# Regrouping the second feed-forward block of a top-k attention kernel, with one matmul reshaped and every rank set anew

## The chip, the cores and the metric

One Trainium2 chip, one of its cores. The metric is the device time of one run in microseconds (us). Five engines work side by side, each through its own list of instructions in a fixed order: PE (matmuls, with weight loads shown as PEld), DVE, ACT, POOL, and SP, which here only issues DMAs.

## The reference, cut to what matters

```python
# q, k, v: (2, 8, 576, 64); 1152 tokens = 9 tiles of 128; d_model 512, d_ff 2048
scores = scale * np.matmul(q, k.transpose(0, 1, 3, 2))
kth = np.partition(scores, -32, axis=-1)[..., -32:-31]
scores = np.where(scores >= kth, scores, -1e9)
attn = softmax(scores)                      # over the 32 that are left
x = np.matmul(attn, v)                      # heads put back: (1152, 512)
h = x @ w_in;  x = (h * np.tanh(softplus(h))) @ w_out      # first block
h = x @ w2_in; out = (h / (1 + np.exp(-h))) @ w2_out       # second block
```

The four weight arrays arrive as float64 and are turned into float32 in the kernel (`convert`), with ACT and POOL; q, k and v are float32.

## The kernel before, in words

The 1152 tokens are nine tiles of 128 rows, and the eight heads are four pairs, so there are 36 pieces of attention (a tile and a head pair), called pairs below and numbered 1 to 36 in the order in which PE turns their weights over. A pair is eight looks for the eight largest scores (L394) and six replacements (L397) on DVE, an exponential on ACT, a mask (L414 on DVE for tiles 0 to 5; L290 or L292 on POOL or DVE for tiles 6 to 8), nine transposes on PE (L439), copies of these out of PSUM (`pt`), and the products with the values (L455 and L457, function `values`). The last chunk of values holds the last 64 keys of each of the two heads, one above the other; a single product with 128 columns (L457) adds it to both heads.

Two feed-forward blocks follow. Each has 16 chunks of `w_in` and 16 of `w_out`. The lists `BLOCK1` and `BLOCK2` say which tiles share a pass over the weights, and how: `'n'` multiplies in float32 as it stands, which the profile shows as two recorded instructions for each product; `'r'` splits each operand into a float32r high part and a rest and adds three products (`passes`). For `'r'` the weights have to be split first (`weight`: a cast L282 or L284 into `ws`, then a subtraction, L290 on POOL or L292 on DVE). The first `'r'` group splits all chunks; some are kept or written to DRAM for the groups behind it, the others are split again by each group. The activations are split by `split_unit`, into a tile named `wide`, a name that the buffers of the float64 weights have too.

What stands when on which engine is not written out. Each step is added to `Plan` with a rank, made from the tables `TILES`, `DUE1`, `DUE2` (when a tile or a group is due), `OFF` (how much earlier or later a kind of step is) and `FLEX`, `FLEX1` (which engine takes a step that two could take). `Plan.emit` takes the steps one by one in the order of rank as their inputs and buffers allow, and so fixes each engine's list. On the chip each engine goes through its list in order and waits where an input is not there yet.

Of the kernel before, what the change touches and what calls it, by code (L numbers as in the profile page):

```python
# [11 lines left out]
F32R = mybir.dt.float32r  # L12
# [14 lines left out]


BLOCK1 = [([0], 'n'), ([1], 'n'), ([2], 'n'), ([3, 4], 'r'), ([5, 6], 'r'), ([7, 8], 'r')]
BLOCK2 = [([0, 1], 'n'), ([2], 'n'), ([3, 4], 'r'), ([5, 6], 'r'), ([7, 8], 'r')]  # L30

TILES = [(19.37, 6.76), (46.36, 14.1), (106.73, 4.63), (204.37, 9.99), (225.06, 11.69), (258.55, 49.85), (345.98,
         18.22), (519.3, 17.23), (461.45, 16.83)]
DUE1 = [(55.53, 32.57), (72.6, 11.18), (185.18, 33.6), (264.74, 3.6), (326.98, 167.36), (749.26, 11.24)]
DUE2 = [(194.98, 61.15), (262.2, 26.21), (504.62, 78.52), (783.18, 203.62), (946.46, 197.95)]

SBUF_BUFS = dict(kraw=1, kk=5, v=5, qraw=2, qs=2, sc=4, rest=1, e=1, pt=2, m8=10, bias=10, den=8, x=3, dt=2, xt=1,
                 wraw=9, ws=8, hs=2, th=1, wide=3, y=2, o=2)
PSUM_BUFS = dict(att=2, misc=1, h=3, y=2)

FLEX = dict(khi=-199.43, klo=-179.86, qhi=-300.0, qlo=65.82, whi=259.95, wlo=-153.31, ghi=-62.92, glo=163.54,
            hs=286.73, mk=-58.0, se=-300.0, den=105.07, y=271.68, sc=-47.47, pt=57.06, dt=-238.16, xlo=98.83)
FLEX1 = dict(khi=245.84, klo=30.36, qhi=-26.57, qlo=179.72, whi=-172.94, wlo=-208.13, ghi=-191.1, glo=300.0, hs=19.48,
             mk=8.23, se=None, den=-282.09, y=None, sc=252.9, pt=None, dt=239.76, xlo=-232.84)
EARLY = 553.02

OFF = dict(kload=578.07, qload=135.46, k=16.71, q=-13.88, sp=314.62, sc=197.87, bias=39.06, e=246.77, tp=342.92,
           pt=330.03, av=-14.23, x=487.41, den=300.22, dw=35.2, dp=222.21, xt=191.17, m=-75.12, cload=96.71,
           cpn=-97.42, cse=5.37, cw=-99.8, cmid=-37.21, wload=572.6, wsplit=-171.63, wstore=206.7, g=-82.77, hs=-40.2,
           y=-31.25, th=709.1)  # L50
# [20 lines left out]
class Plan:  # L71
# [173 lines left out]
def kernel(ctx: ExitStack, tc, qh, kh, va, w1i, w1o, w2i, w2o, out):  # L245
    nc = tc.nc
    NT, DM = out.shape
    NPAIR, D = qh.shape[1], qh.shape[2] // 2
# [94 lines left out]
    def attention(t, p, rank):  # L343
        g, j = group_of[t]
# [3 lines left out]
        pp = parts(t)  # L348
        key = (t, p)
# [99 lines left out]
        def values():  # L449
            av = get(K("av"), lambda: psum("misc", [P, P]))  # L450
            for b, r0, r1 in pp:
                v = T["v", b, p]
                for c in range(NM):
                    for h in range(2):
                        nc.tensor.matmul(av[h * D:h * D + D, r0:r1], lhsT=v[:, h * NM + c, :], rhs=pt()[:, h * (NM + 1) + c, r0:r1],  # L455
                                         start=(c == 0), stop=False, skip_group_check=True)
                nc.tensor.matmul(av[:, r0:r1], lhsT=v[:, 2 * NM:].rearrange("p c e -> p (c e)"), rhs=pt()[:, NM, r0:r1],  # L457
                                 start=False, stop=True, skip_group_check=True)
        add([("pe", 1.35 * len(pp), 0, values)], reads=[K("pt", c) for c in range(0, NB, 3)] + [("v", b, p) for b, _, _ in pp],
            writes=[K("av")], uses=[(K("av"), "ps_misc"), (K("pt"), "pt")] + [(("v", b, p), "v") for b, _, _ in pp],  # L460
            rank=rank + 10.5, boost="av")
        add([("act", 0.11, 0, lambda: nc.scalar.add(den()[:, 0], den()[:, 0], tiny)),
# [182 lines left out]

# [236 lines left out]
```

## Time and profile before

| | |
|---|---|
| Time, median of 3 runs | 653.43 us (652.98 to 654.75) |
| Profiled execution: span from first to last instruction | 654.1 us |
| PE busy | 606.1 us (93%) |
| DVE busy | 539.5 us (82%) |
| ACT busy | 476.3 us (73%) |
| POOL busy | 382.3 us (58%) |
| DMA queue of SP, share of 16 engines | 80.4% |

The profiled execution has no time of its own beside its span; the span is 0.6 us above the median of the runs. Busy shares are means over a program with stages: attention is spread over most of it, and the second block's last groups fill the end. A busy PE may still be a PE that waits inside an instruction, so PE's rate is read from the steps between the starts of its instructions.

### The profile page before, as it was taken

The page shows a single profiled execution, that of the slowest core. Times are in us where ns is not written, and L with a number is a line of the kernel's source. Part 1 is how long each engine was busy: PE and PEld are TensorE (multiplying, and loading weights), DVE is VectorE, ACT ScalarE, POOL GpSimd, SP SyncE. Part 2 cuts the span into 40 slices and gives each one's busy share as a digit, 9 for nine tenths or more (in the row PEclk, how much of TensorE's full clock was granted, in tenths as well). Part 3 has the DMA queues.
Part 4 walks back from the last instruction along what each step waited for, and adds up shares of the span by engine and source line. Part 5 has one row for each costly group of instructions (what it writes and reads, how often), then busy time and mean ns, then how long its engine had stood idle before and what let it go on. Part 6 is the DMA issues. An engine that isn't in the chain of part 4 may idle for free.

```text
span 654.1 us, 13089 instructions
## 1 busy us (share of the span) xinstructions
PE 606.1 (93%) x4536; PEld 537.0 (82%) x4536; DVE 539.5 (82%) x1106; ACT 476.3 (73%) x993; POOL 382.3 (58%) x334
## 2 busy tenths in 40 slices
PE   1298788999999999999999999999999999999997
PEld 1177667999999866668999878999988899999996
DVE  4999999997999999989999979979998234554550
ACT  6799999988699998988978666878777344332321
POOL 6898569761267888987549236556787233322221
PEclk9999967999999999999999999999999999999999
DMA  8987649898789868799999589875876998887752
GB/s 309 293 256 222 197 159 330 312 361 263 204 271 345 276 192 271 268 305 347 389 402 368 151 272 355 316 259 191 272 255 223 374 300 294 278 263 256 246 179 80
DMA packets 85650, 178.34 MB, mean 273 GB/s; under 512 B 8144, under 2 KB 29136, under 8 KB 85584
## 3 DMA queue, kind: packets, MB, share of 16 engines
q1 hardware_dynamic: 85584, 177.50, 80.4%
q8 instruction: 36, 0.59, 0.3%
q14 instruction: 30, 0.25, 0.1%
HBM read 138.94 MB, written 38.54 MB: 271 GB/s over the span
## 4 chain that ended last, share of the span: by engine, by line
PE 53%; DVE 16%; ACT 15%; DMA 7%; issue 4%; POOL 4%; SPq 1%; POOLq 0%; ACTq 0%
PE ps_h L630 20%; PE ps_y L701 12%; PE ps_y L808 11%; DVE m L394 6%; DVE rest L397 5%; ACT ws L505 4%; PE ps_att L378 3%; DMA wraw<-w1i 3%; PE ps_att L439 2%; PE ps_misc L455 2%; ACT wraw L517 2%; ACT pt L282 2%; ACT e L410 2%; DVE e L414 2%; POOL wraw L519 2%
## 5 line engine op out<-in xcount | busy, mean ns | idle before, releaser
L394 DVE MAX8 m<-rest 128x8 f32<-128x576 f32 x216 | 154.4, 745 | 0.1
L397 DVE MATCH_REPLACE8 rest<-m,rest 128x576 f32<-128x576 f32 x144 | 106.2, 741 | 0.0
L509 POOL TENSOR_TENSOR ws<-ws 128x512 int32<-128x512 int32 x64 | 86.7, 1359 | 28.9 <-ACT ws L505 27.2
L378 PE MATMUL ps_att<-kk,qs 128*128 128x288 f32 x320 | 72.8, 346 | 31.6 <-POOL kk L290 24.5
L282 ACT CAST ws<-wraw 128x512 fp32r<-128x512 f32 x93 | 57.4, 621 | 53.8 <-PE ps_h L630 25.3
L519 POOL TENSOR_TENSOR wraw<-wraw,ws 128x512 int32<-128x512 int32 x64 | 85.5, 1346 | 15.9 <-ACT wraw L517 11.0
L505 ACT ACTIVATE ws<-wide,zone 128x512 int32<-128x512 int16 x128 | 94.5, 779 | 0.0
L378 PEld LDWEIGHTS ps_att<-kk,qs 128*128 128x128 f32 x320 | 51.3, 205 | 43.2 <-POOL kk L290 26.0
L292 DVE TENSOR_TENSOR ws<-wraw,ws 128x512 fp32r<-128x512 f32 x65 | 58.9, 924 | 31.3 <-ACT ws L282 30.9
L630 PE MATMUL ps_h<-y,ws 128*128 128x256 f32 x576 | 75.3, 280 | 0.0
L630 PEld LDWEIGHTS ps_h<-y,ws 128*128 128x128 f32 x576 | 73.1, 188 | 2.7
L290 POOL TENSOR_TENSOR ws<-wraw,ws 128x512 fp32r<-128x512 f32 x44 | 57.6, 1318 | 27.3 <-ACT ws L282 14.8
L630 PE MATMUL ps_h<-xt,ws 128*128 128x256 f32 x576 | 72.8, 282 | 0.0
L701 PE MATMUL ps_y<-wide,ws 128*128 128x256 f32 x540 | 71.3, 283 | 0.0
L630 PEld LDWEIGHTS ps_h<-xt,ws 128*128 128x128 f32 x576 | 69.5, 188 | 1.5 <-issue 1.2
L290 POOL TENSOR_TENSOR wide<-th,wide 128x512 fp32r<-128x512 f32 x24 | 31.5, 1313 | 66.7 <-DVE wide L284 65.4
L701 PEld LDWEIGHTS ps_y<-wide,ws 128*128 128x128 f32 x540 | 66.5, 189 | 0.0
L808 PE MATMUL ps_y<-ws,wide 128*128 128x512 f32 x252 | 64.8, 396 | 0.0
L290 POOL TENSOR_TENSOR wide<-hs,wide 128x512 fp32r<-128x512 f32 x24 | 32.0, 1342 | 49.4 <-DVE wide L284 40.2
L439 PE MATMUL ps_att<-ident,e 128*128 128x128 f32 x324 | 52.6, 287 | 6.7 <-DVE e L414 3.9
L701 PE MATMUL ps_y<-hs,wraw 128*128 128x128 f32 x384 | 52.4, 286 | 2.2 <-ACT hs L670 2.2
L394 DVE MAX8 m<-sc 128x8 f32<-128x576 f32 x72 | 52.8, 747 | 1.3 <-ACT sc L282 0.7
(89 smaller groups left out, 1231.5 us busy)
## 6 DMA issues: line engine op xcount, KB each, us to landing
wraw<-w1i SPq DMA_DIRECT2D x64, 256.0 KB, 4.8
wraw<-w2i SPq DMA_DIRECT2D x64, 256.0 KB, 4.0
ws<-w1o_split SPq DMA_DIRECT2D x30, 512.0 KB, 5.1
ws<-w2o_split SPq DMA_DIRECT2D x28, 512.0 KB, 4.4
wraw<-w1o SPq DMA_DIRECT2D x48, 256.0 KB, 5.8
wide<-in_w1i_dram SPq DMA_DIRECT2D x16, 512.0 KB, 5.6
wide<-in_w1o_dram SPq DMA_DIRECT2D x16, 512.0 KB, 5.0
wide<-in_w2i_dram SPq DMA_DIRECT2D x16, 512.0 KB, 5.1
```

Of the source, the lines that this page charges most:

```text
L282: ways.append(("act", act_us(n, psum), act, lambda: nc.scalar.copy(get_out(), get_in())))
L290: ways.append(("pool", pool_us(n), pool, lambda: nc.gpsimd.tensor_tensor(out=get_out(), in0=get_a(), in1=get_b(), op=op)))
L378: nc.tensor.matmul(o, lhsT=l, rhs=r[:, f * SH:(f + 1) * SH], start=(i == 0), stop=(i == len(ops) - 1))
L394: add([("dve", 0.67, 0, lambda i=i, h=h, src=src: nc.vector.max(out=m8()[:, h, 8 * i:8 * i + 8], in_=src()[:, h]))], reads=srck, writes=[K ...
L397: add([("dve", 0.73, 0, lambda i=i, h=h, src=src: nc.vector.match_replace(out=rest()[:, h], in_to_replace=m8()[:, h, 8 * i:8 * i + 8], in_ ...
L439: nc.tensor.transpose(o[:, i, :], ef[:, (c + i) * P:(c + i + 1) * P], ident)
L505: add([("act", act_us(UNIT) + 0.14, 0, lambda i=i: nc.scalar.activation(pn()[:, i], top(), AF.Relu, scale=ONE16 - 2 * ONE16 * i, bias=zone))],
L509: ways = [("pool", pool_us(UNIT), 0, lambda: nc.gpsimd.tensor_tensor(out=se(), in0=pn()[:, 0], in1=pn()[:, 1], op=ALU.subtract))]
L519: add([("pool", pool_us(UNIT), 0, lambda: nc.gpsimd.tensor_tensor(out=w().bitcast(I32), in0=w().bitcast(I32), in1=se(), op=ALU.add))], rea ...
L630: nc.tensor.matmul(hp[:, c, :], lhsT=l, rhs=rr, start=(i == 0), stop=(i == len(ops) - 1))
L701: nc.tensor.matmul(yp[:, o, :], lhsT=l[:, d * P:(d + 1) * P], rhs=rr[:, c, :], start=(fc == 0 and k == 0 and o == 0), stop=last, skip_grou ...
L808: nc.tensor.matmul(op, lhsT=gg[:, c, i * P:(i + 1) * P], rhs=wt, start=(fc == 0 and k == 0), stop=(fc == NFC - 1 and k == len(ops) - 1))
```

## The change

Tile 0 goes through the second block alone, in plain float32; tiles 1 and 2, of which 1 was in a plain pair with tile 0 and 2 was alone and plain, become a pair in three float32r products. The last chunk of values is multiplied as two products of 64 columns. The split activations get three buffers of their own, named `g`, so that `wide` only holds weights as they arrive; the space comes from a smaller scratch area. All tables of ranks are new numbers, and with them every engine's order and the choice of engine for steps that two can take.

```diff
-BLOCK2 = [([0, 1], 'n'), ([2], 'n'), ([3, 4], 'r'), ([5, 6], 'r'), ([7, 8], 'r')]
+BLOCK2 = [([0], 'n'), ([1, 2], 'r'), ([3, 4], 'r'), ([5, 6], 'r'), ([7, 8], 'r')]
...
-DUE2 = [(194.98, 61.15), (262.2, 26.21), (504.62, 78.52), (783.18, 203.62), (946.46, 197.95)]
+DUE2 = [(109.32, 182.94), (461.87, 43.54), (680.53, 120.97), (1247.47, 545.08), (3221.42, 579.84)]
...
-                 wraw=9, ws=8, hs=2, th=1, wide=3, y=2, o=2)
+    wraw=9, ws=8, hs=2, th=1, wide=3, g=3, y=2, o=2)
...
-FLEX = dict(khi=-199.43, klo=-179.86, qhi=-300.0, qlo=65.82, whi=259.95, wlo=-153.31, ghi=-62.92, glo=163.54,
+FLEX = dict(khi=-2892.29, klo=-904.54, qhi=-1532.65, qlo=2296.17, whi=696.95, wlo=1977.98, ghi=1637.18,
...
-                nc.tensor.matmul(av[:, r0:r1], lhsT=v[:, 2 * NM:].rearrange("p c e -> p (c e)"), rhs=pt()[:, NM, r0:r1],
-                                 start=False, stop=True, skip_group_check=True)
+                for h in range(2):
+                    nc.tensor.matmul(av[h * D:h * D + D, r0:r1], lhsT=v[:, 2 * NM + h, :], rhs=pt()[:, NM, r0:r1],
+                                     start=False, stop=True, skip_group_check=True)
...
-        hi = lambda: get(key, lambda: sbuf("wide", [P, 2 * UNIT + 2], F32R)[:, :2 * n].rearrange(
-            "p (t n) -> p t n", t=2))[:, 0]
+        hi = lambda: get(key, lambda: sbuf("g", [P, 2, UNIT], F32R)[:, :, :n])[:, 0]
...
-    nc = _bacc.Bacc("TRN2", target_bir_lowering=False, num_devices=1)
+    nc = _bacc.Bacc("TRN2", target_bir_lowering=False, num_devices=1, dynamic_dma_scratch_size=1024)
```

The order moves at three places that the prediction speaks of. The first is the start of DVE's list, up to the first pair's first look for the largest scores. Before:

```order
L284 COPY sc<-ps_att 128x288 x2
L394 MAX m_141<-sc 128x8
L284 COPY sc<-ps_att 128x288
L397 MATCH_REPLACE rest<-m_141,sc 128x576
L394 MAX m_141<-sc 128x8
L394 MAX m_141<-rest 128x8
```

and in the changed kernel:

```order
L286 CAST kk<-kraw 128x576
L294 TENSOR_TENSOR kk<-kraw,kk 64x576
L286 CAST qs<-qraw 128x256
L294 TENSOR_TENSOR kk<-kraw,kk 64x576
L286 COPY sc<-ps_att 128x288
L396 MAX m_130<-sc 128x8
```

DVE now splits part of the first keys and queries itself (`kk`, `qs`), where ACT and POOL did all of it, and takes one score copy ahead of its first look where it took two.

The second place is PE's list where the second block begins (`ps_h<-y` is its first product, `ps_y<-hs` and `ps_h<-xt` belong to the first block, `kk,qs` and `ident,e` to attention). Before:

```order
L630 MATMUL ps_h<-xt,wraw 128x128 x4
L630 MATMUL ps_h<-y,wraw 128x256 x4
L378 MATMUL ps_att<-kk,qs 128x288 x4
L630 MATMUL ps_h<-xt,wraw 128x128 x4
L630 MATMUL ps_h<-y,wraw 128x256 x4
L630 MATMUL ps_h<-xt,wraw 128x128 x16
L630 MATMUL ps_h<-y,wraw 128x256 x4
L701 MATMUL ps_y<-hs,wraw 128x128 x4
```

and in the changed kernel:

```order
L633 MATMUL ps_h<-xt,wraw 128x128 x4
L380 MATMUL ps_att<-kk,qs 128x288 x2
L633 MATMUL ps_h<-y,wraw 128x128 x4
L633 MATMUL ps_h<-xt,wraw 128x128 x8
L441 MATMUL ps_att<-ident,e 128x128 x3
L633 MATMUL ps_h<-xt,wraw 128x128 x4
L441 MATMUL ps_att<-ident,e 128x128 x6
L633 MATMUL ps_h<-xt,wraw 128x128 x4
```

Before, the first product of the second block stands behind the transposes of 13 pairs, with 256 columns for tiles 0 and 1; now it stands behind those of eight, with 128 columns for tile 0.

The third place is where the weights of a split group have their rests subtracted. Before, near the end, DVE does it between its other work:

```order
L292 TENSOR_TENSOR ws<-wraw,ws 128x512
L788 SCALAR_TENSOR_TENSOR th<-th,ps_h 128x512
L292 TENSOR_TENSOR ws<-wraw,ws 128x512
L284 CAST wide<-th 128x512
L292 TENSOR_TENSOR ws<-wraw,ws 128x512
```

and in the changed kernel POOL does it, here for tiles 1 and 2, right behind the last conversion of weights (`wraw<-wraw,ws`):

```order
L522 TENSOR_TENSOR wraw<-wraw,ws 128x512
L292 TENSOR_TENSOR ws<-wraw,ws 128x512 x3
L292 TENSOR_TENSOR xt<-x,xt 128x128
L292 TENSOR_TENSOR ws<-wraw,ws 128x512 x3
L292 TENSOR_TENSOR qs<-qraw,qs 128x256
L292 TENSOR_TENSOR ws<-wraw,ws 128x512 x2
L292 TENSOR_TENSOR g<-th,g 128x512
```

All 65 such subtractions leave DVE; POOL has 125 of them where it had 44.

## Rows read from the trace of the kernel before

**Rows 1.** Busy time of each engine in five stretches of the span

```profile
0.00:120.00 120.00, 81.24 (x534) 68.75 (x535) 109.32 (x234) 108.09 (x226) 92.89 (x83) 0.93 0.78 253
120.00:270.00 150.00, 147.12 (x1166) 127.98 (x1166) 145.24 (x319) 135.51 (x281) 99.02 (x93) 1.00 0.83 276
270.00:387.00 117.00, 115.24 (x884) 98.75 (x883) 109.93 (x231) 90.35 (x198) 71.73 (x63) 1.00 0.90 316
387.00:510.00 123.00, 122.14 (x959) 111.19 (x959) 113.26 (x236) 95.15 (x217) 80.77 (x68) 1.00 0.80 274
510.00:655.00 145.00, 140.32 (x1003) 130.30 (x999) 61.74 (x89) 47.23 (x74) 37.95 (x30) 1.00 0.73 247
```

**Rows 2.** The chain of waits, pieces at several places: start us, us, what

```profile
18.92 1.32 DVE m L394 x2
27.64 1.46 DVE rest L397 x2
...
299.02 1.72 PE ps_y L808 x4
...
397.02 0.86 PE ps_y L808 x2
397.87 1.41 PE ps_h L630 x12
...
571.80 1.40 PE ps_y L808 x6
573.19 1.41 PE ps_h L630 x12
```

**Rows 3.** Timeline of PE, near 145, 212 and 386 us: start, us, what

```profile
144.24 1.09 PE L455 MATMUL ps_misc<-pt,v 128*64 128x128 f32 x16
145.26 0.49 PE L457 MATMUL ps_misc<-pt,v 128*128 128x128 f32 x2
145.59 1.61 PE L701 MATMUL ps_y<-hs,wraw 128*128 128x128 f32 x13
...
212.75 1.89 PE L630 MATMUL ps_h<-y,wraw 128*128 128x256 f32 x8
214.48 0.72 PE L701 MATMUL ps_y<-hs,wraw 128*128 128x128 f32 x5
...
386.15 0.82 PE L439 MATMUL ps_att<-ident,e 128*128 128x128 f32 x6
```

**Rows 4.** Timeline of all engines, the first 10 us

```profile
3.60 1.48 ACT L282 CAST kk<-kraw 128x576 fp32r<-128x576 f32 x2 [1.60 <-DMA kraw<-in_kh_dram]
4.41 2.76 POOL L290 TENSOR_TENSOR kk<-kraw,kk 64x576 fp32r<-64x576 f32 x2 [3.09 <-DMA kraw<-in_kh_dram]
7.25 1.41 POOL L290 TENSOR_TENSOR qs<-qraw,qs 128x256 fp32r<-128x256 f32 x2
8.67 0.94 DVE L284 COPY sc<-ps_att 128x288 f32<-128x288 f32 x2 [8.67 <-PE ps_att L378]
9.64 0.76 DVE L394 MAX8 m<-sc 128x8 f32<-128x576 f32 x1
```

**Rows 5.** Who DVE waited for from 270 to 387 us: total, times, longest

```profile
DVE sc L284 <- PE ps_att L378: 3.8, 3, 2.0
DVE x L480 <- PE ps_misc L457: 1.1, 2, 0.6
```

**Rows 6.** Timeline of DVE and POOL, near 23 and 293 us

```profile
22.99 1.81 DVE L414 SCALAR_TENSOR_TENSOR e<-sc,m,e 128x576 f32<-128x576 f32 x1
...
22.40 1.78 POOL L509 TENSOR_TENSOR ws<-ws 128x512 int32<-128x512 int32 x1
...
292.88 0.80 DVE L414 SCALAR_TENSOR_TENSOR e<-sc,m,e 128x576 f32<-128x576 f32 x1
```

**Rows 7.** Groups by line, whole span: count, busy us, mean ns, idle before

```profile
L414 DVE SCALAR_TENSOR_TENSOR e<-sc,m,e 128x576 f32<-128x576 f32 x48 | 48.1, 1028 | 0.8 <-ACT e L410 0.8
L292 DVE TENSOR_TENSOR ws<-wraw,ws 128x512 fp32r<-128x512 f32 x65 | 58.9, 924 | 31.3 <-ACT ws L282 30.9
L292 DVE TENSOR_TENSOR xt<-x,xt 128x128 fp32r<-128x128 f32 x14 | 8.7, 625 | 2.4 <-ACT xt L282 2.4
L292 DVE TENSOR_TENSOR e<-sc,e 128x576 f32<-128x576 f32 x6 | 5.2, 882 | 1.1 <-ACT e L420 1.1
L284 DVE COPY dt<-ps_att 128x128 f32<-128x128 f32 x6 | 1.7, 286 | 2.7 <-PE ps_att L471 2.6
L284 DVE COPY pt<-ps_att 128x384 f32<-128x384 f32 x2 | 1.1, 546 | 1.1 <-PE ps_att L439 1.1
L290 POOL TENSOR_TENSOR ws<-wraw,ws 128x512 fp32r<-128x512 f32 x44 | 57.6, 1318 | 27.3 <-ACT ws L282 14.8 <-DMA wraw<-w1i 3.1 <-DVE ws L284 2.9
```

**Rows 8.** Timeline, the end of the span

```profile
648.76 1.56 PE L808 MATMUL ps_y<-keep,wide 128*128 128x512 f32 x6
649.65 1.30 ACT L821 ACTIVATE o<-ps_y 128x512 f32<-128x512 f32 x2 [9.37 <-PE ps_y L808]
650.27 1.04 SPq L823 DMA_DIRECT2D out_dram<-o  x2
```

More of the change, by code (lines that the diff above doesn't have):

```diff
@@ L29 @@
 BLOCK1 = [([0], 'n'), ([1], 'n'), ([2], 'n'), ([3, 4], 'r'), ([5, 6], 'r'), ([7, 8], 'r')]
-BLOCK2 = [([0, 1], 'n'), ([2], 'n'), ([3, 4], 'r'), ([5, 6], 'r'), ([7, 8], 'r')]
-TILES = [(19.37, 6.76), (46.36, 14.1), (106.73, 4.63), (204.37, 9.99), (225.06, 11.69), (258.55, 49.85), (345.98,
-         18.22), (519.3, 17.23), (461.45, 16.83)]
-DUE1 = [(55.53, 32.57), (72.6, 11.18), (185.18, 33.6), (264.74, 3.6), (326.98, 167.36), (749.26, 11.24)]
-DUE2 = [(194.98, 61.15), (262.2, 26.21), (504.62, 78.52), (783.18, 203.62), (946.46, 197.95)]
+BLOCK2 = [([0], 'n'), ([1, 2], 'r'), ([3, 4], 'r'), ([5, 6], 'r'), ([7, 8], 'r')]
@@ L37 @@
+TILES = [(45.87, 13.3), (119.97, -8.62), (159.6, -6.03), (191.54, 9.56), (175.63, 19.64), (283.14, -10.0),
+    (273.36, -16.1), (905.15, 4.27), (314.25, -4.46)]
+DUE1 = [(-273.89, 63.61), (102.84, 100.7), (218.37, 63.14), (634.39, 8.23), (661.9, 30.84), (1187.11, 12.24)]
+DUE2 = [(109.32, 182.94), (461.87, 43.54), (680.53, 120.97), (1247.47, 545.08), (3221.42, 579.84)]
 SBUF_BUFS = dict(kraw=1, kk=5, v=5, qraw=2, qs=2, sc=4, rest=1, e=1, pt=2, m8=10, bias=10, den=8, x=3, dt=2, xt=1,
-                 wraw=9, ws=8, hs=2, th=1, wide=3, y=2, o=2)
+    wraw=9, ws=8, hs=2, th=1, wide=3, g=3, y=2, o=2)
@@ L39 @@
 PSUM_BUFS = dict(att=2, misc=1, h=3, y=2)
-FLEX = dict(khi=-199.43, klo=-179.86, qhi=-300.0, qlo=65.82, whi=259.95, wlo=-153.31, ghi=-62.92, glo=163.54,
[L42 to L50, printed above, removed]
+FLEX = dict(khi=-2892.29, klo=-904.54, qhi=-1532.65, qlo=2296.17, whi=696.95, wlo=1977.98, ghi=1637.18,
+    glo=-126.15, hs=280.65, mk=-2834.51, se=345.2, den=4890.98, y=4541.93, sc=3398.49, pt=-4016.38, dt=956.63,
+    xlo=655.68)
@@ new lines @@
+FLEX1 = dict(khi=-1800.74, klo=957.1, qhi=890.66, qlo=-2866.6, whi=1499.07, wlo=-227.96, ghi=-4613.42,
+    glo=1715.94, hs=-2857.57, mk=-114.15, se=None, den=739.33, y=None, sc=372.06, pt=None, dt=3303.09,
+    xlo=225.36)
+EARLY = -1307.04
+OFF = dict(kload=1692.95, qload=1528.2, k=-1684.93, q=1068.22, sp=1645.37, sc=2289.39, bias=-2052.9, e=2435.58,
+    tp=2034.48, pt=2466.99, av=1518.03, x=1889.89, den=2843.68, dw=-84.49, dp=1165.65, xt=-734.6, m=2409.58,
+    cload=1080.72, cpn=-3803.37, cse=-6018.75, cw=-254.7, cmid=1741.39, wload=6319.47, wsplit=-2858.61,
+    wstore=4829.76, g=-2302.13, hs=-245.91, y=932.59, th=1865.48)
@@ L456, in values @@
                                          start=(c == 0), stop=False, skip_group_check=True)
-                nc.tensor.matmul(av[:, r0:r1], lhsT=v[:, 2 * NM:].rearrange("p c e -> p (c e)"), rhs=pt()[:, NM, r0:r1],
-                                 start=False, stop=True, skip_group_check=True)
-        add([("pe", 1.35 * len(pp), 0, values)], reads=[K("pt", c) for c in range(0, NB, 3)] + [("v", b, p) for b, _, _ in pp],
+                for h in range(2):
+                    nc.tensor.matmul(av[h * D:h * D + D, r0:r1], lhsT=v[:, 2 * NM + h, :], rhs=pt()[:, NM, r0:r1],
+                                     start=False, stop=True, skip_group_check=True)
+        add([("pe", 1.25 * len(pp), 0, values)], reads=[K("pt", c) for c in range(0, NB, 3)] + [("v", b, p) for b, _, _ in pp],
             writes=[K("av")], uses=[(K("av"), "ps_misc"), (K("pt"), "pt")] + [(("v", b, p), "v") for b, _, _ in pp],
@@ L581, in weight @@
         add(copy_ways(UNIT, hi, lambda: T[wk], dve="whi", twice=True), reads=[wk], writes=[sk + (0,)], uses=U,
-            rank=rank - 6, boost="wsplit")
+            rank=rank - (6 if g else 2), boost="wsplit")
         add(tt_ways(UNIT, lo, lambda: T[wk], hi, ALU.subtract, dve="wlo"), reads=[wk, sk + (0,)],
-            writes=[sk + (1,)], uses=U, rank=rank - 6, boost="wsplit")
+            writes=[sk + (1,)], uses=U, rank=rank - (6 if g else 2), boost="wsplit")
         if where == "dram" and g == first:
@@ L634, in split_unit @@
     def split_unit(key, n, U, src, skeys, suses, r):
-        hi = lambda: get(key, lambda: sbuf("wide", [P, 2 * UNIT + 2], F32R)[:, :2 * n].rearrange(
-            "p (t n) -> p t n", t=2))[:, 0]
-        add(copy_ways(n, hi, src, dve="ghi", twice=True), reads=skeys, writes=[key + (0,)], uses=suses + [(key, "wide")],
+        hi = lambda: get(key, lambda: sbuf("g", [P, 2, UNIT], F32R)[:, :, :n])[:, 0]
+        add(copy_ways(n, hi, src, dve="ghi", twice=True), reads=skeys, writes=[key + (0,)], uses=suses + [(key, "g")],
             rank=r, boost="g")
         add(tt_ways(n, lambda: T[key][:, 1], src, hi, ALU.subtract, dve="glo"), reads=skeys + [key + (0,)],
-            writes=[key + (1,)], uses=suses + [(key, "wide")], rank=r, boost="g")
-        return ([key + (0,), key + (1,)], [(key, "wide")],
+            writes=[key + (1,)], uses=suses + [(key, "g")], rank=r, boost="g")
+        return ([key + (0,), key + (1,)], [(key, "g")],
                 lambda: tuple(T[key][:, i].rearrange("p (u n) -> p u n", u=U) for i in range(2)))
```

## The prediction

> **What bounds the kernel now.** I read the busy times by stretch first [rows 1]. Two engines are close to full: DVE is busy 109.32 + 145.24 + 109.93 = 364.5 of the first 387 us, so it idles 22.5 us there, and PE is busy nearly all of every stretch from 120 us on. From 510 us DVE has 61.74 us of work in 145 us, and PE alone sets the pace. A busy PE says little of its rate, so I took the rate from the steps in the chain [rows 2]: a float32r product of 256 columns takes 1.41 / 12 = 0.118 us, one of 512 columns 1.40 / 6 = 0.233, a plain float32 product of 512 columns two recorded instructions of 0.43. The pieces of the chain lie end to end at these places: there PE is dense.
>
> One instant ties the two engines together: the transposes of a pair. PE can't start them before DVE has masked that pair, and everything behind them in PE's list comes later. The transposes of pair 28 begin at 386.15 us [rows 3], and the last matmul group ends at 648.76 + 1.56 = 650.3 [rows 8]: 264 us later. Added up by the steps above, PE's list behind pair 28 holds 263.4 us of work, so PE does not wait there any more. Then 3.8 us follow to the end of the span for the last copies and the store (they begin at 649.65 and 650.27) [rows 8]. So the span is DVE's work up to pair 28 (about 364), plus DVE's idle time up to there (22.5), plus 264, plus 3.8: 654.1, the profiled execution, 0.6 above the median of the runs.
>
> **The change, part by part.**
>
> *PE's work.* Tiles 0 and 1 as a plain pair were 128 recorded instructions of 256 columns at (214.48 - 212.75) / 8 = 0.216 us [rows 3] and 64 of 512 columns at 0.43: 27.6 + 27.5 = 55.1 us. Tile 2 alone was 128 of 128 columns (0.112: half of 0.216 and a little) and 32 of 512: 28.1. Now tile 0 alone costs these 28.1, and the pair of tiles 1 and 2 costs 192 products at 0.118 and 96 at 0.233: 45.0. Saved: 83.2 - 73.1 = 10.1 us. Values: 16 recorded products of 64 columns take 145.26 - 144.24 = 1.02 us, 0.064 each, and the two of 128 columns behind them 0.33 [rows 3]. Four more of 0.064 in their place save 0.07 us, 32 times, and a little more on the eight half-width ones of tile 4: 3 us. The bounds are +13 (each new product as dear as the old one, 40 times 0.33) and -6 (the old one's 0.33 down to half); I take -3, since the row of the same shape is the nearest. In sum PE has 13 us less to do.
>
> *Where PE's saving lies.* In the new order PE's list ahead of pair 28 is shorter, but behind it is not. Behind it stand 96 more float32r products of the first block (96 x 0.118 = 11.3), and seven fewer plain ones of 512 columns in two halves (7 x 0.86 = 6.0), eight fewer score products (1.1), and the cheaper values (0.7): 3.5 us more. So the 13 us, and those 3.5, are saved ahead of pair 28, where DVE is what PE waits for.
>
> *DVE's work up to pair 28*, from its list. Gone: 18 subtractions of weights, 8 of `xt`, 8 casts of weights, six score copies and five smaller ones. New: 28 copies of `pt`, 15 of `dt`, 5 mask subtractions, seven casts of queries, and four casts and three subtractions of keys. Looks and replacements step 0.66 and 0.73 us [rows 2], 0.08 below what single ones last, so I price the others by their means [rows 7] less 0.08: gone 18 x 0.84 + 8 x 0.55 + about 9.5 = 29 us, new 28 x 0.47 + 15 x 0.21 + 5 x 0.80 + about 8 = 28. Nothing is gained or lost, to 1 us. Up to pair 20 it is 15 us more, from the copies of `pt` and `dt`, given back by pair 28.
>
> *DVE's idle time up to pair 28.* (a) The start: the first look is at 9.64 us, since the scores wait for the rests of keys and queries, which POOL makes one behind another: 4.41 to 7.2 the keys, from 7.25 the queries [rows 4]. Now DVE makes keys' rests itself and POOL begins with the queries. Four DVE steps of some 0.4 to 0.8 us from 3.6 on end near 6.2; PE's second product can start near 6.3 in place of 8.0, and the first look comes near 7.6. DVE is then 2 us earlier with 2 us more done: 4 us of idle time gone (bounds 0 and 5). (b) From 270 to 387 DVE idles 7.07 us [rows 1], and 4.9 of them are waits for PE's scores and values [rows 5], since PE was the later one there. The new list leaves PE 361 us behind pair 20 (before 383), so there PE is early and waits for DVE; I take the 5 us as gone (bounds 0 and 7).
>
> *The rest.* POOL gets 81 more subtractions of weights at 1.318 us [rows 7], and 16 chunks more are split in all, because the pair of tiles 1 and 2 is now the first split group of four. POOL's list up to pair 28 grows from 255 to 303 us, 79% of the time: hidden as long as POOL is not late, and 0 in the sum. What its cover is worth is the third rival. Behind 510 us POOL had 37.95 of 145 us [rows 1] and has room. ACT swaps copies of `pt` for casts of about the same length: 0. DMA: 14 more loads of 512 KB, 16 fewer of 256 KB, 2% more, on a queue whose share was 0.73 to 0.90 [rows 1]: 0. Three buffers for `g` remove waits of the casts on weight loads: 0, as PE never waits for them there.
>
> *The sum.* 654.1 + 0 (DVE's work) + 3.5 (PE behind pair 28) - 4 (start) - 5 (waits for PE) = 648.6 for the span, 0.6 less for the median: **648.0**.
>
> *A rule against it.* DVE's mask takes 0.80 us at 292.88, and 1.81 us at 22.99 while a POOL subtraction that began at 22.40 lasts 1.78 [rows 6]; the mean is 1.028 [rows 7]. The Trainium skill, SBUF — State Buffer, section "Who interferes with whom", says that a DVE instruction with two SBUF inputs contends with a GpSimd instruction that reads SBUF, and that whoever is first keeps the shared port for its whole instruction. The trace agrees: 0.80 against 1.81. By the mean row nothing is added; by that rule, with POOL busier, the sum would be some 9 us higher, as the third rival works out from rows.
>
> **The rivals.**
>
> 1. *PE sets the end throughout*, and its 13 us come out whole: 654.1 - 13.1 = 641, median 640.4. For it: PE is busy 30 us of 30 in most of the second half, and tile 0's own second block gives it work from pair 8 on, where it idled 38.8 of the first 120 us [rows 1]. Against it: DVE's work ahead of pair 28 is the same.
>
> 2. *The gain doesn't come.* The first look stays near 9.6, or DVE meets new waits of the same size, and idles 19 to 22 us: 652 to 655. For it: in 120 to 270 us DVE idles only 4.8 us now, hard to better, and a new order has new waits.
>
> 3. *POOL holds DVE up: slower.* Up to pair 28 DVE has 57 instructions with two SBUF inputs (48 masks, 6 mask subtractions, 3 of keys). They now wait 1.03 - 0.80 = 0.23 us each, with POOL busy 263.6 of 387 us. If at 79% each meets a POOL instruction of 1.3 us half-way whenever POOL is busy, the wait is 0.79 x 0.66 = 0.52 and 17 us are added; half of that, 8.5, gives 657. It decides from a mean mask of about 1.11 us on. Against it: 27 subtractions that could wait as well have left DVE's list.
>
> **How the numbers follow.** A change within 0.3% (2 us) is about what a measurement here can't tell from none. My forecast, 644 to 651.4, has 0.42; the first rival with what lies below 644, 0.17; the second (651.5 to 655.4) 0.18; the third and other new waits above that, 0.23. So faster 0.59, same 0.18, slower 0.23. For 8 in 10 the range goes from 637, a little under the first rival, to 659, a little over the third's middle; the forecast's own range is 644 to 651.4.
>
> **What would show it.** Right: the first look near 7.6 us; the transposes of pair 28 near 377 to 380 us, with PE dense behind them for 267 us; masks at a mean near 1.0; POOL busy near 445 us in all; a row of two 64-column products in 0.13 us. Wrong: a mean mask over 1.1, waits of DVE for ACT or POOL of more than 10 us in the middle third, or waits of PE for split weights (`ws`) from POOL, which would add to PE behind pair 28. If PE still idles behind pair 28, the tie at that place was the wrong one, and the split of weights is the first suspect.

## The result and the profile after

The changed kernel takes **664.75 us** (median; 663.19 to 664.99), beside it the kernel before 654.09: ratio **1.0148 [1.0127, 1.017]**. It is 1.5% slower, and the interval lies clear of 1; 648.0 was forecast, and the range ended at 659. The profiled execution spans 662.8 us and took 664.61. Three of ten runs of one version below (halves and casts together) were some 1.7% longer at a lower granted clock, and its time leaves them out.

Busy time by stretches in the changed kernel, as [rows 1]: stretch, length, then PE, PEld, DVE, ACT and POOL with their instructions, granted clock, DMA share, GB/s.

```profile
0.00:120.00 120.00, 73.58 (x496) 61.49 (x497) 112.02 (x229) 101.96 (x196) 96.42 (x85) 0.87 0.80 258
120.00:270.00 150.00, 140.16 (x1210) 122.35 (x1209) 148.31 (x317) 137.01 (x276) 116.71 (x105) 0.99 0.91 311
270.00:387.00 117.00, 111.41 (x900) 100.78 (x900) 116.78 (x242) 98.11 (x223) 104.11 (x89) 0.99 0.81 284
387.00:510.00 123.00, 123.00 (x1064) 116.89 (x1064) 112.05 (x245) 93.17 (x214) 80.17 (x72) 1.00 0.80 272
510.00:663.00 153.00, 149.08 (x1052) 138.22 (x1048) 52.76 (x71) 53.48 (x83) 58.00 (x43) 0.99 0.73 243
```

DVE is busy 377.1 of the first 387 us, 12.6 more than in [rows 1]. From 120 to 387 us it hardly idles, 1.9 us, while PE, nearly full there before, idles 15.4. POOL is busy 317.2 of the 387 us; it was 263.6.

The timeline at the transposes of pair 28 and at the end of the span, as [rows 3, 8]:

```profile
392.79 0.82 PE L441 MATMUL ps_att<-ident,e 128*128 128x128 f32 x6
...
657.53 1.54 PE L810 MATMUL ps_y<-keep,g 128*128 128x512 f32 x6
658.43 1.28 ACT L823 ACTIVATE o<-ps_y 128x512 f32<-128x512 f32 x2 [7.07 <-PE ps_y L810]
659.06 1.02 SPq L825 DMA_DIRECT2D out_dram<-o  x2
```

Pair 28 comes at 392.79, where 386.15 stood and 377 was forecast. From there to the last matmul's end (659.07) it is 266.3 us, then 3.7 to the end of the span. The tie that the prediction used holds; what comes ahead of it is late. PE's waits over the whole span say for what (total, times, longest). Before:

```profile
PE ps_att L378 <- POOL kk L290: 24.5, 3, 9.8
PE ps_att L439 <- DVE e L414: 3.9, 4, 2.6
```

and in the changed kernel:

```profile
PE ps_att L441 <- DVE e L416: 20.3, 14, 4.6
PE ps_att L380 <- POOL kk L292: 11.7, 1, 11.7
```

The transposes (L439, L441) wait 20.3 us for masks, where they waited 3.9.

Groups by line on DVE, as [rows 7]:

```profile
L416 DVE SCALAR_TENSOR_TENSOR e<-sc,m,e 128x576 f32<-128x576 f32 x48 | 59.7, 1271 | 0.1
L286 DVE COPY pt<-ps_att 128x384 f32<-128x384 f32 x41 | 21.9, 545 | 1.3 <-PE ps_att L441 1.1
L286 DVE CAST qs<-qraw 128x256 fp32r<-128x256 f32 x9 | 5.5, 616 | 0.1
L286 DVE CAST kk<-kraw 128x576 fp32r<-128x576 f32 x4 | 3.8, 950 | 3.8 <-DMA kraw<-in_kh_dram 3.8
L294 DVE TENSOR_TENSOR kk<-kraw,kk 64x576 fp32r<-64x576 f32 x3 | 3.2, 1071 | 0.1
L286 DVE CAST qs<-qraw 128x128 fp32r<-128x128 f32 x3 | 2.6, 880 | 0.0
```

The 48 masks, all ahead of pair 28, take 59.7 us where they took 48.1 [rows 7]. The timeline of DVE, and then of POOL, near 106 us shows why:

```profile
105.97 0.96 DVE L416 SCALAR_TENSOR_TENSOR e<-sc,m,e 128x576 f32<-128x576 f32 x1
...
106.86 1.81 DVE L416 SCALAR_TENSOR_TENSOR e<-sc,m,e 128x576 f32<-128x576 f32 x1
...
105.03 1.28 POOL L522 TENSOR_TENSOR wraw<-wraw,ws 128x512 int32<-128x512 int32 x1
106.27 3.53 POOL L512 TENSOR_TENSOR ws<-ws 128x512 int32<-128x512 int32 x2
```

A mask alone lasts 0.80. The first one here starts under a POOL instruction that ends at 106.31, and ends 0.62 later; POOL's next one, starting at 106.27, has to wait for that mask, and the second mask waits for it: 1.81 us. The two POOL instructions take 3.53 together, where one alone lasts 1.28. Each engine holds the other up in turn.

### The profile page after: what moved, and what is told of

Its sections match the earlier page's. It is cut to its first block, busy times and chain, and to the rows that moved or that the text cites. A ratio compares the mean times of both kernels' runs of the same rounds, so it can differ in the third digit from the quotient of the medians.

```text
span 662.8 us, 13541 instructions
## 1 busy us (share of the span) xinstructions
PE 597.2 (90%) x4712; PEld 539.7 (81%) x4712; DVE 541.9 (82%) x1100; ACT 483.7 (73%) x990; POOL 455.4 (69%) x391
## 4 chain that ended last, share of the span: by engine, by line
PE 56%; DVE 23%; ACT 11%; DMA 4%; POOL 2%; issue 2%; SPq 0%; DVEq 0%; ACTq 0%
PE ps_h L633 21%; PE ps_y L810 12%; PE ps_y L703 10%; DVE m L396 7%; DVE rest L399 7%; DVE e L416 5%; PE ps_att L380 4%; PE ps_misc L457 3%; ACT ws L508 3%; PE ps_att L441 3%; ACT wraw L520 2%; ACT e L412 1%; DMA w1o<-wraw 1%; DVE pt L286 1%; DMA wide<-in_w2o_dram 1%
## 5 line engine op out<-in xcount | busy, mean ns | idle before, releaser
L292 POOL TENSOR_TENSOR ws<-wraw,ws 128x512 fp32r<-128x512 f32 x125 | 166.3, 1343 | 83.1 <-DVE ws L286 38.4
L633 PE MATMUL ps_h<-y,ws 128*128 128x256 f32 x768 | 100.0, 280 | 0.0
L633 PEld LDWEIGHTS ps_h<-y,ws 128*128 128x128 f32 x768 | 96.7, 188 | 3.6 <-issue 0.3
L512 POOL TENSOR_TENSOR ws<-ws 128x512 int32<-128x512 int32 x64 | 86.3, 1359 | 18.3 <-ACT ws L508 17.4
L810 PE MATMUL ps_y<-ws,g 128*128 128x512 f32 x336 | 88.3, 402 | 0.0
L441 PE MATMUL ps_att<-ident,e 128*128 128x128 f32 x324 | 56.3, 299 | 27.2 <-DVE e L416 20.3
L441 PEld LDWEIGHTS ps_att<-ident,e 128*128 128x128 f32 x324 | 39.3, 151 | 40.1 <-DVE e L416 14.3
L703 PE MATMUL ps_y<-g,ws 128*128 128x256 f32 x540 | 70.4, 281 | 0.0
L810 PEld LDWEIGHTS ps_y<-ws,g 128*128 128x128 f32 x336 | 60.5, 190 | 11.1
L703 PEld LDWEIGHTS ps_y<-g,ws 128*128 128x128 f32 x540 | 66.2, 188 | 0.2 <-issue 0.2
L416 DVE SCALAR_TENSOR_TENSOR e<-sc,m,e 128x576 f32<-128x576 f32 x48 | 59.7, 1271 | 0.1
L284 ACT COPY sc<-ps_att 128x288 f32<-128x288 f32 x137 | 49.9, 403 | 10.8 <-PE ps_att L380 10.6
```

What stands on the lines that cost most here:

```text
L292: ways.append(("pool", pool_us(n), pool, lambda: nc.gpsimd.tensor_tensor(out=get_out(), in0=get_a(), in1=get_b(), op=op)))
L416: add([("dve", 0.73, 0, lambda h=h: nc.vector.scalar_tensor_tensor(out=e()[:, h], in0=sc()[:, h], scalar=m8()[:, h, TOPK - 1:TOPK], in1=e( ...
L441: nc.tensor.transpose(o[:, i, :], ef[:, (c + i) * P:(c + i + 1) * P], ident)
L512: ways = [("pool", pool_us(UNIT), 0, lambda: nc.gpsimd.tensor_tensor(out=se(), in0=pn()[:, 0], in1=pn()[:, 1], op=ALU.subtract))]
L633: nc.tensor.matmul(hp[:, c, :], lhsT=l, rhs=rr, start=(i == 0), stop=(i == len(ops) - 1))
L703: nc.tensor.matmul(yp[:, o, :], lhsT=l[:, d * P:(d + 1) * P], rhs=rr[:, c, :], start=(fc == 0 and k == 0 and o == 0), stop=last, skip_grou ...
```

## The experiments

Theory 1: POOL's instructions hold DVE's masks and casts, DVE's work up to pair 28 is longer by that, and all behind pair 28 is late by it. The main rival: the new order or grouping is worse in itself. Each run stands beside runs of the kernel before on the same chip (medians 654.74, 655.68 and 655.49 in the three groups), and the ratios are against those. Single figures of pair 28 and of DVE's work up to it are from the one profiled execution of each kernel.

**The mask with a single SBUF input**, in both kernels. It takes as long as a mask that isn't held; it leaves the masking out.

```diff
-nc.vector.scalar_tensor_tensor(out=e()[:, h], in0=sc()[:, h], scalar=m8()[:, h, TOPK - 1:TOPK], in1=e()[:, h],
-                               op0=ALU.is_ge, op1=ALU.mult, accum_out=den()[:, 0, h])
+nc.vector.tensor_scalar(out=e()[:, h], in0=e()[:, h], scalar1=m8()[:, h, TOPK - 1:TOPK], scalar2=None,
+                        op0=ALU.max, op1=ALU.add, accum_out=den()[:, 0, h])
```

In the changed kernel, expected: 

> The changed kernel with the same edit (the mask reads one tensor and does not mask; attention runs over all keys), same order on all engines. Theory 1: the mean mask falls from 1.27 to about 0.80 us, 23 us of DVE's work, and the kernel comes to 642 to 650, within 4 us of the kernel before with the same edit, so that the holding of masks is most of the 10.7 us lost. Rival (the new order as such, with its copies of attention weights on DVE and PE's waits, is what costs): both kernels gain alike, and this one stays 8 to 11 us above the other.

In the kernel before, expected: 

> The kernel before, with one edit: the mask of tiles 0 to 5 on DVE reads one tensor (the exponentials) where it read two (scores and exponentials); it does not mask, so attention runs over all keys. Same order on all engines. Theory 1 (POOL's instructions hold DVE's two-input masks): the mean mask falls from 1.03 to about 0.80 us, 48 times, 11 us of DVE's work, of which 5 to 9 us show in the end: 645 to 649. Rival (the mask is as long as it is because of its own work): mask stays near 1.03, time within 2 us of 654.

Measured: changed kernel 647.65 us, 0.9908 [0.9874, 0.9943]; kernel before 652.09, 0.9954 [0.993, 0.9977]. The group of masks in the kernel before with this mask, then the group of masks, the transposes of pair 28, and the first two stretches of the changed kernel with it:

```profile
L414 DVE TENSOR_SCALAR_CACHE_REDUCE e<-e,m 128x576 f32<-128x576 f32 x48 | 37.3, 804 | 0.7 <-ACT e L410 0.7
```

```profile
L416 DVE TENSOR_SCALAR_CACHE_REDUCE e<-e,m 128x576 f32<-128x576 f32 x48 | 37.1, 801 | 0.1
```

```profile
376.31 0.82 PE L441 MATMUL ps_att<-ident,e 128*128 128x128 f32 x6
```

```profile
0.00:120.00 120.00, 76.80 (x538) 65.50 (x540) 107.47 (x239) 105.68 (x204) 95.94 (x88) 0.86 0.87 277
120.00:270.00 150.00, 143.21 (x1260) 127.30 (x1257) 147.41 (x331) 140.08 (x288) 116.19 (x110) 1.00 0.93 321
```

Masks lose 22.6 us, pair 28 comes 16.5 earlier, the span is 16.4 shorter and the time 17.1 less. In the kernel before they lose 10.8 (37.3 are left), but the time is only 2.7 less, of 654.74, where 5 to 9 were expected: pair 28 comes 3.6 earlier there, at 382.57, and DVE idles 5.7 us more up to it. With the hold gone from the masks of both, the changed kernel is 4.4 us faster by the medians and 3 by the ratios, whose intervals touch: some 3 to 4 us of the regrouping and the new order come out. The granted clock of the first stretch, 0.87 where [rows 1] have 0.93, isn't the cause: it is 0.86 here.

**POOL that only writes.** If POOL is the holder, the masks must shorten when it is DVE's code that stays as it is. A fill (`memset`) writes a constant and reads no tensor.

```diff
+    def write_only(o):
+        for c in (UNIT, UNIT, UNIT // 2):
+            nc.gpsimd.memset(o[:, :c], 0.001)
...
-            ways.append(("pool", pool_us(n), pool, lambda: nc.gpsimd.tensor_tensor(out=get_out(), in0=get_a(), in1=get_b(), op=op)))
+                if n == UNIT:
+                    write_only(o.bitcast(F32))
...
+        ways = [("pool", pool_us(UNIT), 0, lambda: write_only(se().bitcast(F32)))]
...
+            add([("pool", pool_us(UNIT), 0, lambda: write_only(w()))],
```

Expected: 

> The changed kernel, every list in its order, but every GpSimd subtraction and addition of 128x512 (the split of weights and activations, both steps of the conversion) is replaced by three fills of about the same length together (0.52 + 0.52 + 0.3 us), which write and read nothing; the weights are left out by it. Theory 1, POOL's reads hold DVE's two-input instructions and casts: the mean mask falls from 1.27 to 0.80 to 0.90 us (only the small subtractions for queries and keys are left to hold it), the transposes of pair 28 come at 375 to 380 us, the time is 645 to 651. Rival, the new order itself makes DVE late and masks are long for another reason: masks stay above 1.15 us and the time at 658 or above. The granted clock has to be looked at, since the data are other ones.

Measured: 648.59 us, 0.9898 [0.9871, 0.9925]. Groups by line on DVE, and the transposes of pair 28:

```profile
L426 DVE SCALAR_TENSOR_TENSOR e<-sc,m,e 128x576 f32<-128x576 f32 x48 | 38.9, 839 | 0.1
...
L286 DVE CAST qs<-qraw 128x256 fp32r<-128x256 f32 x9 | 3.5, 391 | 0.2
L286 DVE CAST kk<-kraw 128x576 fp32r<-128x576 f32 x4 | 1.8, 452 | 3.8 <-DMA kraw<-in_kh_dram 3.8
L286 DVE CAST qs<-qraw 128x128 fp32r<-128x128 f32 x3 | 0.9, 289 | 0.0
```

```profile
374.49 0.82 PE L451 MATMUL ps_att<-ident,e 128*128 128x128 f32 x6
```

POOL is as busy as before this edit (456.1 us against 455.4), the order is the same, and every mask is the two-input one; what POOL reads is gone, and its instructions are shorter, 0.53 us in place of 1.27. The masks fall to 0.84 us. That is no matter of shorter instructions: only three masks last over 0.82, and each of these meets a subtraction of keys or queries, which still reads. The casts of keys and queries fall from 11.9 us in all to 6.2. So the casts are held too, which the prediction hadn't counted. The clock isn't the cause: it is 0.979 over the span against 0.970, and behind pair 28 PE takes 267.4 us, no less than before this edit.

**The kernel before with a busier POOL**, the same cause from the other side.

```diff
+        def pool_se():
+            nc.gpsimd.tensor_tensor(out=se(), in0=pn()[:, 0], in1=pn()[:, 1], op=ALU.subtract)
+            if T.get("conv", 0) % 3:
+                nc.gpsimd.tensor_tensor(out=pn()[:, 1], in0=se(), in1=pn()[:, 1], op=ALU.subtract)
```

Expected: 

> The kernel before with POOL's first conversion step issued twice for two chunks of three (43 more instructions of 1.36 us, 58 us, into an operand that nobody reads any more). POOL is then busy some 327 of the first 386 us, as in the changed kernel. Theory 1: the mean mask goes from 1.03 to 1.15 to 1.3 us, DVE has 6 to 13 us more up to pair 28, and the time is 657 to 664, though the order is that of before. Rival: a busier POOL costs DVE nothing, masks stay below 1.08 and the time at 653 to 656.

Measured: 713.49 us, 1.089 [1.0865, 1.0914]. The group of masks, and two waits over the whole span (total, times, longest):

```profile
L414 DVE SCALAR_TENSOR_TENSOR e<-sc,m,e 128x576 f32<-128x576 f32 x48 | 61.7, 1309 | 4.0 <-ACT e L410 4.0
```

```profile
PE ps_att L378 <- POOL kk L290: 33.0, 4, 12.7
...
PE ps_h L633 <- POOL wraw L522: 18.3, 10, 3.7
```

The masks came out at 1.309, just above what was expected, in the old order: a busier POOL alone makes them long, without the new ranks. The time did not come out: 58 us more of POOL made POOL itself late, and PE waits for its keys (33.0 us, 24.5 before) and weights (18.3 and 8.1 in the two largest groups, 0.5 in all before). This run tells nothing of what 13.6 us more of masks cost.

**Values as two 64-column products, in the kernel before**, in the old order.

```diff
-nc.tensor.matmul(av[:, r0:r1], lhsT=v[:, 2 * NM:].rearrange("p c e -> p (c e)"), rhs=pt()[:, NM, r0:r1],
+for h in range(2):
+    nc.tensor.matmul(av[h * D:h * D + D, r0:r1], lhsT=v[:, 2 * NM + h, :], rhs=pt()[:, NM, r0:r1],
```

Expected: 

> The kernel before with the last chunk of values as two 64-column products, its planned cost and all orders kept. Theory 1: PE has 3 us less to do, but only the nine pairs from 28 on lie where PE sets the pace: 0.7 us, 653.4, the same within the interval. Rival (PE sets the end throughout): 3 us less, 651.

Measured: 654.46 us, 0.9998 [0.9982, 1.0015]: the same. What these products save on PE doesn't come out as long as DVE sets pair 28.

**The new grouping with the old tables.** The kernel changed as a whole, but for the tables of ranks.

```diff
-DUE2 = [(109.32, 182.94), (461.87, 43.54), (680.53, 120.97), (1247.47, 545.08), (3221.42, 579.84)]
+DUE2 = [(110.0, 80.0), (300.0, 60.0), (504.62, 78.52), (783.18, 203.62), (946.46, 197.95)]
...
```

(`TILES`, `DUE1`, `FLEX`, `FLEX1`, `EARLY` and `OFF` as before.) Expected: 

> The changed kernel's grouping, values and split buffers with the tables of the kernel before, except the due times of its two first groups of the second block, (110, 80) and (300, 60). Theory 1: the grouping is not at fault; with the old choice of engines DVE has the weights' subtractions again and POOL fewer, masks stay near 1.05 us and the time is 645 to 656. Rival (the grouping itself costs, by its 16 more chunks to split and its first split group in the middle of attention): 660 to 668, as the changed kernel.

Measured: 718.83 us, 1.099 [1.0939, 1.1041]. Both theories missed the time; the masks are at 0.987, with POOL busy 251 of the first 387 us. In its second stretch PE is busy 117 of 150 us:

```profile
120.00:270.00 150.00, 117.33 (x836) 99.97 (x835) 127.42 (x275) 124.82 (x244) 111.31 (x99) 0.83 0.77 259
```

The first two due times were set by hand here, and nobody tuned the order for this grouping. Whether that is what costs over 60 us is not shown, so grouping and ranks can't be told apart in this way.

**The mask on ACT**, in both kernels: ACT makes dropped scores hugely negative and takes the exponential of that.

```diff
-nc.vector.scalar_tensor_tensor(out=e()[:, h], in0=sc()[:, h], scalar=m8()[:, h, TOPK - 1:TOPK], in1=e()[:, h],
-                               op0=ALU.is_ge, op1=ALU.mult, accum_out=den()[:, 0, h])
+nc.scalar.mul(bias()[:, 0, h], m8()[:, h, TOPK - 1:TOPK], FAR)
+nc.scalar.activation(e()[:, h], sc()[:, h], AF.Prelu, bias=bias()[:, 0, h], scale=-FAR, alpha=1 / FAR)
+nc.scalar.activation(e()[:, h], e()[:, h], AF.Exp, scale=-scale, accum_out=den()[:, 0, h])
```

Expected, changed kernel: 

> The changed kernel, with the mask taken from DVE for tiles 0 to 5: ACT makes scores below the 32nd largest hugely negative (one pass of 576) and takes the exponential of that with its sum. The result is the reference's. DVE loses 48 masks (59.7 us), ACT gets some 48 times 0.75 more (36 us, 484 to 520). Theory 1: nothing is left on DVE for POOL to hold in the first 24 pairs but casts and keys; the copies and looks are single-input, so pair 28 comes no later than with the single-input mask (376.3) and the time is 640 to 647, faster than both kernels. Rival: ACT, which now waits for the last look of each pair, holds up the casts behind it and the time is 652 or above.

Expected, kernel before: 

> The kernel before with the same mask on ACT. DVE loses 48.1 us. PE has 606 us of work against 597 in the changed kernel. Theory 1: 645 to 652, some 4 to 8 us above the changed kernel with the same mask, since the regrouping's saving on PE shows once DVE is not held up. Rival (the regrouping or the order is worse in itself): not slower than the changed kernel with the same mask.

Measured: 728.09 us, 1.1112 [1.1089, 1.1134], and 724.8, 1.1036 [1.1, 1.1072]. DVE was relieved and ACT became what DVE and PE wait for most, as the first run's rival said, far beyond its bound. The second run's rival came true as well: the kernel before isn't slower than the changed one with this mask. Waits in the changed kernel with this mask:

```profile
DVE den L470 <- ACT den L466: 76.9, 20, 7.3
...
PE ps_att L442 <- ACT e L414: 54.0, 26, 7.0
```

**POOL's conversion in halves**, if a hold lasts one POOL instruction.

```diff
-nc.gpsimd.tensor_tensor(out=se(), in0=pn()[:, 0], in1=pn()[:, 1], op=ALU.subtract)
+for c in (0, UNIT // 2):
+    nc.gpsimd.tensor_tensor(out=se()[:, c:c + UNIT // 2], in0=pn()[:, 0, c:c + UNIT // 2],
+                            in1=pn()[:, 1, c:c + UNIT // 2], op=ALU.subtract)
```

(and the conversion's addition likewise.) Expected, changed kernel: 

> The changed kernel, with POOL's 128 conversion instructions of 128x512 each issued as two of 128x256 (0.2 us more for a pair of halves, some 25 us more of POOL). In the changed kernel instructions of these two kinds hold 21 masks, 13 us beyond 0.80 in all. Theory 1 with a hold of one whole POOL instruction: the wait for such a one halves, the mean mask falls from 1.27 to 1.10 to 1.17, and the time to 655 to 661, if the longer POOL isn't late itself. Rival (DVE waits until POOL has nothing more to do): masks stay at 1.22 or above and the time at 663 or above.

Expected, kernel before: 

> The kernel before with the conversion in halves on POOL. Seventeen masks meet conversions there, some 9 us in all. Theory 1: mean mask from 1.03 to 0.92 to 0.97, and the time at 651 to 655, since with the mask of one input, 10.8 us less of masks gave only 2.6. Rival (POOL's longer list is late, as in the run with doubled conversion steps): 660 or above.

Measured: 662.99 us, 1.0117 [1.0076, 1.0158]; and 669.06, 1.017 [1.0095, 1.0245]. The timeline of the changed kernel with halves, DVE and then POOL:

```profile
107.80 1.11 DVE L416 SCALAR_TENSOR_TENSOR e<-sc,m,e 128x576 f32<-128x576 f32 x1
...
108.85 1.27 DVE L416 SCALAR_TENSOR_TENSOR e<-sc,m,e 128x576 f32<-128x576 f32 x1
...
108.25 3.14 POOL L514 TENSOR_TENSOR ws<-ws 128x256 int32<-128x256 int32 x3
```

A mask held by a half lasts 1.27, by a whole instruction 1.81: the hold goes with the length of POOL's instruction. But the mean mask is 1.264, as without the edit, and the time is at the rival's bound. Sorted by the POOL instruction that a mask meets first, the masks under conversions lost 13.2 us in the changed kernel; with halves they lose 7.2 and, in a single mask of 6.34 us (below), 5.5 more. So both are there: the step of theory 1, and in one mask what the rival said.

In the kernel before, the masks did not fall to 0.92 to 0.97 but rose to 1.143, and pair 28 comes at 401, 15 us later. POOL being late doesn't explain it: PE waits 18.0 us for keys from POOL up to there, less than the 24.5 without halves, but 14.6 us for masks, where it was 3.9:

```profile
PE ps_att L378 <- POOL kk L290: 18.0, 2, 9.6
PE ps_att L439 <- DVE e L414: 14.6, 7, 5.6
```

DVE's work up to pair 28 is 10.3 us longer, and two of its instructions lost more than that, a mask and a subtraction of `xt` that is otherwise done in some 0.4 us:

```profile
107.39 6.22 DVE L414 SCALAR_TENSOR_TENSOR e<-sc,m,e 128x576 f32<-128x576 f32 x1
...
297.52 6.47 DVE L292 TENSOR_TENSOR xt<-x,xt 128x128 fp32r<-128x128 f32 x1
```

Each of them lasts while ten POOL instructions run.

**Casts of keys and queries on ACT**, alone and with the halves.

```diff
-lambda: nc.vector.tensor_copy(get_out(), get_in())
+early = nc.scalar.copy if dve in ("khi", "qhi") else nc.vector.tensor_copy
```

Expected: 

> The changed kernel with DVE's casts of keys and queries (14 up to pair 28, 10.2 us there) issued on ACT at the same place of the program. Theory 1: DVE's work up to pair 28 falls by 10 us, the masks stay near 1.27, the time is 654 to 660. Rival (the first look hangs on these casts, or ACT holds other casts behind them): 662 or above.

Expected with the halves: 

> Both edits of the two runs before at once: halves of the conversion on POOL, casts of keys and queries on ACT. Theory 1: the gains add, 16 us of DVE's work up to pair 28, of which PE lets 12 come out: 648 to 655, faster than the kernel before. Rival (POOL, with 25 us more, becomes what is late): 660 or above.

Measured: 663.07 us, 1.0104 [1.0068, 1.0139], and 662.00, 1.0091 [1.0058, 1.0125], both as the rivals said. DVE's steps up to pair 28 are 8.4 us less with the casts moved, but pair 28 comes only 2.1 earlier. DVE idles 6 us more, most of it in small pieces spread over 30 to 270 us; two of its waits up to pair 28:

```profile
DVE den L470 <- ACT den L466: 3.2, 4, 1.2
...
DVE pt L287 <- PE ps_att L442: 2.2, 3, 1.3
```

In the changed kernel the first of these is 0.5 us and the second isn't there. So most of the work taken from DVE was given back as waits, somewhat over half of them for ACT itself; whether a late ACT stands behind PE's part too is not shown. No version here beats the kernel before with the whole computation done.

## Why the prediction was wrong, by its own steps

**The tie was right, and so was everything behind it.** PE needs 266.3 us behind pair 28 (264.2 before and 3.5 more, 267.7, forecast) and the tail is 3.7.

**The step that failed is DVE's work up to pair 28, "nothing is gained or lost, to 1 us".** It is some 19 us more: added up by the steps from one DVE instruction to the next, 364.2 us before, 383.1 after. The exchange of kinds was right: 28 copies of `pt` step 0.465 us each (0.47 forecast), 18 of `dt` 0.20. What was mis-sized is what POOL does to the others. The masks, at nothing in the sum, are 11.8 us dearer by these steps. The new casts of keys and queries cost 9.2 us where the sum had some 5.6, and the keys' subtractions are 0.8 dearer. What left DVE's list was worth 25.4 us, not 29: its subtractions of weights stepped 0.74, not 0.84. That makes 19.7; mask subtractions and copies came 1.5 cheaper, and 0.7 us is left over. The run with the fills shows how much of the changed kernel's 383.1 is POOL's hold: there the same list steps 356.5 us, 26.6 less; masks are 20.9 less and the casts 6.1 (10.2 down to 4.1).

The sum with what was measured: 648.6 + 18.9 (DVE's work) - 3.2 (DVE idles 9.7 us up to pair 28, where 21.9 less the 9 of the prediction, 12.9, was forecast) - 1.4 (PE behind pair 28) - 0.1 (rounding) = 662.8, the span. The step from span to median adds 2.5: the median lies 1.9 above this span (the profiled execution took 1.8 more than its span), where the prediction took 0.6 below. A median of three runs and the span of a single other execution were no basis for that 0.6.

**The third rival is what happened.** Its mechanism was priced at 0.52 us of wait for each two-input instruction in full and at half of the extra 17 us as its middle. The masks wait 1.271 - 0.80 = 0.47, close to full. Its deciding point, a mean mask of 1.11, was passed. Its price in full gives 648.0 + 17 = 665; the half had no row behind it, and it was the half that kept the range at 659. That the full price lands on 664.75 is partly luck: POOL is busy 317 of 387 us, not 303, and casts, which have one input, were left out of its count of 57. The rule of the Trainium skill that stood beside it (SBUF — State Buffer, section "Who interferes with whom") says that casts can enter a mode that takes the shared port as well; the trace agrees, with 616 against 391 ns for a 128x256 cast. It also sets apart the form that writes an accumulator, and the single-input mask, which does, is not held: 801 ns under a POOL as busy.

**DVE's idle time: right, in other places.** The first look comes at 8.46 us (7.6 forecast, 9.64 before): the keys' second subtraction is done at 6.14, then DVE waits 1.76 us for PE. Up to there DVE idles some 3 us less, not 4. From 270 to 387 us it idles 0.2 us, where 5 of 7.07 were to go, and from 120 to 270 another 3 are gone. So the new order does keep DVE fed; it fills it with longer instructions.

**PE's saving lies ahead of pair 28, as forecast, and is hidden there.** With the hold gone the changed kernel comes to 648.59 and 647.65 us, where the forecast was 648.0. This agreement is partly chance: in the run with the fills DVE's work is 356.5 us, less than the 364 of the forecast, and its idle time 18.0, more than 12.9. Of 13 us of PE's work some 3 to 4 come out even then, by the two runs with the single-input mask. The 13 themselves are not shown: PE is busy 597.2 us in all, 8.9 less than before. The first rival, PE alone, is out. The reshaped values, forecast at 0.13 us for two products, take 0.16 at the place shown: four step 0.32 us, as long as the two that they replace (0.33 [rows 3]).

```profile
143.58 0.39 PE L460 MATMUL ps_misc<-pt,v 128*64 128x128 f32 x4
143.90 0.33 PE L474 MATMUL ps_att<-ident,x 128*128 128x128 f32 x1
```

Which of POOL's work holds the masks can be counted from the timelines, by the POOL instruction that a held mask meets first. Before, 14 masks lose 8.0 us under conversions; in the changed kernel 18 lose 13.2, though POOL has as many conversions as before. The subtractions of split weights and activations, of which POOL has more now (56 of weights up to pair 28, 13 before), held no mask before; now they hold four for 6.1 us, 4.0 of it in one mask (below). Keys and queries hold about 3 us in both. So about half of the extra loss is under the work that was moved to POOL. Why conversions meet more masks, and longer, is not settled; the new order is one candidate.

## What to carry to other kernels

Work moved to an engine with idle time isn't free if its instructions hold up those of the engine that bounds the kernel: price each two-input instruction of the bounding engine at half of one instruction of the other times that engine's busy share, take the price in full, and count the casts too. Here that estimate is 0.64 (half of 1.28) x 0.82 = 0.52 us for a mask, with 0.47 measured; for the kernel before it is 0.64 x 0.68 = 0.44, with 0.23 measured, so it can be nearly twice too high. A group's mean (1.028 us) with a free minimum of 0.80 already told that over a fifth was waiting, and that a busier POOL would most likely raise it. And taking work off the engine that bounds helps only where its new home is idle and nobody waits behind it: the mask on ACT gave back more than it took away, the casts on ACT some three quarters.

## What was not expected of the hardware

A waiting mask doesn't always get its turn when POOL's instruction ends. Near 304 us in the changed kernel, DVE and then POOL:

```profile
304.33 4.82 DVE L416 SCALAR_TENSOR_TENSOR e<-sc,m,e 128x576 f32<-128x576 f32 x1
...
303.54 1.29 POOL L292 TENSOR_TENSOR g<-th,g 128x512 fp32r<-128x512 f32 x1
304.79 1.29 POOL L292 TENSOR_TENSOR keep<-wraw,keep 128x512 fp32r<-128x512 f32 x1
306.04 2.49 POOL L292 TENSOR_TENSOR ws<-wraw,ws 128x512 fp32r<-128x512 f32 x2
```

Four POOL instructions run one behind the other, each at its free length, and the mask ends 0.62 us after the last: it lost 4 us at once. At 106 us POOL's next instruction waited for the mask instead. In the run with halves a mask was passed by nine POOL instructions:

```profile
92.04 6.34 DVE L416 SCALAR_TENSOR_TENSOR e<-sc,m,e 128x576 f32<-128x576 f32 x1
```

It isn't rare bad luck: the same mask is passed by the same four instructions in all four versions that keep the changed kernel's masks and its POOL work at that place (4.69 to 4.83 us), and every version with halves has one or two more instructions passed by nine or ten, those of the kernel before above among them. The kernel before has none. What decides it is open.
